# Estimates of the last chunk kept in SBUF, four of its products moved to ScalarE, and buffers and due times set anew

## The chip, the core and the metric

The kernel runs on one core of one Trainium2 chip. The metric is the device time of one execution in microseconds (us), as the median of several runs; a profiled execution gives the trace beside it. The engines are TensorE (PE), VectorE (DVE), ScalarE (ACT) and GpSimd (POOL); SyncE (SP) issues most DMAs here, POOL issues some. The on-chip memories are SBUF and PSUM; matmuls write to PSUM, and GpSimd works on SBUF here.

## The reference

Three stages on 12480 tokens of 128 channels:

```python
h   = mab(I, x)                      # softmax attention of 32 inducing points over all tokens
x1  = mab(x, h)                      # each token attends to the 32 results
h   = x1 @ w_in;  g = max(h, 0) + alpha * min(h, 0)
x2  = g @ w_out                      # first layer, 2048 wide
h   = x2 @ w_in2                     # second layer, 2048 wide
P   = a[0] + a[1]*h + a[2]*h*h + a[3]*h*h*h
Q   = 1 + |b[0]|*|h| + |b[1]|*h*h
out = (P / (Q + 1e-6)) @ w_out2
```

## The kernel before

The attention and the conversion of the weights fill the first 90 us or so; after that the work is cut into 26 chunks of 480 tokens (`W`), and each chunk into 8 units (`NU`), a unit being two blocks of 128 of the 2048 hidden channels, so a tile of 128x960. There are 208 units, numbered `k`; unit 200 is the first of the last chunk, and two units make a pair `j`. For each chunk the first layer runs on PE (`la1`, line 788; `lb`, line 801) with a relu on ACT (`r`, line 793), one chunk ahead of the second layer.

The second layer's rational function of unit `k` is a chain over four engines:

- PE: `l2` computes h into one of two PSUM buffers (lines 842 to 844, six matmuls).
- ACT: `s` = h*h (line 854). POOL: `A` = a3*s + a1 (line 863), and for a pair `B` = a2*s + a0 (line 868).
- DVE: `m` = h*A (line 875). For the pair POOL then issues a DMA, `P`, that adds B to m in SBUF (line 879); m is then the numerator.
- ACT: `z` = |b0*h| in place in PSUM (line 859). DVE: `q` = |b1|*s + z, into a tile `z` in SBUF (line 888): the denominator less a constant.
- ACT: `rho` = 1/sqrt(Q) (line 892) and `r0` = rho*rho (line 897), an estimate of 1/Q, into a PSUM tile `r` that exists once.
- DVE: one Newton step in place in the z tile, `ee` = Q*r0 (line 907), `r1` = (2 - ee)*r0 (line 911).
- POOL: `g` = m*z (line 922). For the last unit of each chunk DVE does it itself, as `g0` and `g` (lines 917 and 924).
- PE: `o` multiplies by the second weights (line 936) into the output of the chunk, which goes out by ACT, PE and a DMA at the chunk's end (`oa`, `ot`, `oy`, lines 948, 955, 962).

The order in which instructions are issued on each engine is fixed when the program is built. `graph` lists every operation with its engine, an assumed duration (`COST`), what it waits for, and a due time made from the table `DUE`; `arranged` then picks, engine by engine, what starts next. So a number in `DUE` changes nothing but the order. Before the first of these orders, a hand-written list (`START`) interleaves attention, conversion and the first chunk's first layer. The conversion of the weights (`cv`: lines 365, 369, 376 and 382, four steps on DVE for each of 16 pieces of 128x512, of which 13 steps are left over for the planned part) works in SBUF in the pool `cvr`. The pool `zz` takes over that memory, so a tile of `zz` can first be written when the last conversion step is done; the denominators z are tiles of `zz`, the numerators m (five buffers of a pair) are tiles of `ew`.

Of the kernel before, what the change touches and what calls it, by code (L numbers as in the profile page):

```python
# [43 lines left out]
DUE = dict(
    x2f=-0.45, la=-9.06, span=2.97, lb1=-13.61, at=-97.53, o=-23.76, o1=-13.46, ot=22.31, pack=12.69,
    l2=(29.67, 35.58, -79.83, -40.1, -11.09, -27.3, -24.5, -43.29),
    s=(-17.84, -32.0, -16.83, -26.56, -59.46, -97.25, -31.04, -54.94),
    A=(-63.73, -120.71, -103.15, -88.14, -48.47, -71.46, -128.35, -89.09),
    m=(-108.75, -22.15, -116.09, -46.72, -47.13, -42.75, -50.15, -148.19),
    B=(-54.95, -120.41, -105.91, -26.76, 36.86, -21.45, -83.45, 36.32),  # L50
    P=(187.3, 56.68, 20.63, 25.06, 67.81, -5.11, 38.88, -25.19),
    z=(-26.7, -63.52, -31.2, -26.94, 5.39, 24.47, 11.89, 15.71),
    q=(32.02, 39.1, 47.63, 65.87, 13.6, 133.96, 50.31, 70.75),
    rho=(36.83, 86.45, 150.83, 117.66, 71.04, 81.94, 112.77, 38.48),
    r0=(78.33, 29.52, 26.2, -49.91, 50.51, 19.63, -30.96, -28.81),
    ee=(62.9, 108.52, 89.98, 43.06, 77.86, 74.23, 43.3, 78.62),
    g0=(70.57, 75.02, 1.99, 84.61, 105.19, 73.56, 80.62, 149.83),
    g=(58.94, 3.2, 116.11, 8.69, 83.04, 10.67, 31.27, 107.91),
    r1=(40.2, 67.74, 21.19, 94.45, -8.56, 116.72, 111.67, -32.38),
    gp=(89.99, 44.35, 54.18, 117.38, 95.33, 178.76, 75.12, 95.23),  # L60
)
SLACK = 0.1
DVE_G = (7,)
MBUFS, ZBUFS = 5, 5
O_GATE, LB_GATE = 1, 6


def graph(NC, NU, due):
# [8 lines left out]
    LATER = ("r",)  # L77
    add(("x2a", 0), "A", C["cp"], [], 0)
    add(("x2b", 0), "V", 0.66, [("x2a", 0)], 0)
    for i in range(4):  # L80
# [4 lines left out]
    add(("w2l", 3), "G", 1.25, [], 1)
    for c in range(NC):
        at = c * CT
        x2 = at - due["x2f"]
# [13 lines left out]
        for j in range(2 * NU if c else 0):  # L102
            p, i = NU * c + j // 2, j % 2
            n = 2 * p + i
            t = x2 - (2 * NU - j) * TU / 2 * due["span"] - due["la"]
            add(("la1", p, i), "P", C["la1"], [("as_", c)], t, take="h1")
            add(("r", p, i), "A", C["r"], [("la1", p, i), ("lb", (n - 10) // 2, n % 2)], t + 0.3, give="h1")
# [3 lines left out]
            add(("lb", p, i), "P", C["lb"] + end, [("r", p, i)] + gate, t, take=None if j else "acc")  # L111
# [104 lines left out]
def tile_induced_attention__prelu_moe__rational_moe(  # L216
# [598 lines left out]
    def x2_f(c):  # L815
        xf = pools["rp2"].tile([P, W], F32, tag="xf", name="xf")
# [56 lines left out]
    def dve_m(k):  # L873
        Mm[k] = pair(MP, "ew", "m", MBUFS, k)
# [227 lines left out]
```

## Time and profile before

| | |
|---|---|
| median of 3 runs | 1214.61 us (1213.43 to 1216.71) |
| profiled execution | 1214.42 us, of which the span from first to last instruction is 1212.6 us |
| PE, ACT, DVE, POOL busy | 95%, 89%, 85%, 84% of the span |
| mean granted TensorE clock | 0.993 of full speed |

A busy share is a mean over stages that differ. In the rows further down a duration stands behind the start of an instruction, both in us from the span's start; what stands in square brackets is the idle time of the engine just before it and the instruction that ended it.

### The profile page before, as it was taken

Reading aid. Unit: us, or ns where it says so; the run is one execution under the profiler, and the core shown is the slowest. Engines: PE = TensorE matmul, PEld = TensorE weight load, DVE = VectorE, ACT = ScalarE, POOL = GpSimd, SP = SyncE. Lnnn points to the kernel's source line nnn. Section 1 sums busy time; section 2 is a strip of 40 time slices with the busy share of each in tenths; the row PEclk is TensorE's granted clock in tenths of the full one; section 3 lists DMA queues with packets and bytes.
Section 4 is the critical chain, followed back from the end, with each engine's and each line's share of the span. In section 5 each row is a group of like instructions: output and inputs, shape, how many; then the busy total and the mean of one; then the engine's idle time right before and its main releaser. Section 6 shows DMA issues by size and latency. Waiting matters only on the chain.

```text
span 1212.6 us, 12428 instructions
## 1 busy us (share of the span) xinstructions
PE 1150.4 (95%) x4137; PEld 685.3 (57%) x4137; DVE 1036.0 (85%) x1006; ACT 1073.9 (89%) x1485; POOL 1017.7 (84%) x693
## 2 busy tenths in 40 slices
PE   4998989999999999999999999999999999999996
PEld 3654555555655565655566555556555655565553
DVE  1796988889888888888988888998889889888996
ACT  3667989999989999999999999999999999999974
POOL 0135988998899998899989899988999898889895
PEclk9998999999999999999999999999999999999998
DMA  9801455454535545544554554454455545444553
GB/s 225 264 1 33 99 106 105 95 105 98 105 78 106 106 98 107 106 86 86 106 106 98 106 106 94 90 103 97 98 106 105 106 91 105 99 91 96 106 106 73
DMA packets 25260, 124.23 MB, mean 102 GB/s; under 512 B 2428, under 2 KB 6812, under 8 KB 24684
## 3 DMA queue, kind: packets, MB, share of 16 engines
q0 software_dynamic: 14976, 102.24, 42.2%
q1 hardware_dynamic: 9410, 18.25, 5.3%
q10 hardware_dynamic: 810, 2.95, 1.0%
q8 instruction: 33, 0.54, 0.2%
q14 instruction: 31, 0.25, 0.1%
HBM read 14.80 MB, written 6.39 MB: 17 GB/s over the span
## 4 chain that ended last, share of the span: by engine, by line
PE 60%; POOL 15%; DVE 9%; ACT 8%; issue 3%; DMA 3%; POOLq 0%; SPq 0%; ACTq 0%
PE oa L936 20%; PE xa L801 15%; POOL m L922 6%; PE h L842 5%; PE h L788 5%; PE h L844 5%; PE h L843 5%; POOL a L863 4%; POOL b L868 4%; DVE m L875 3%; ACT s L854 2%; DMA xs<-in_x_dram 2%; DVE z L888 2%; ACT r L897 2%; DVE z L907 2%
## 5 line engine op out<-in xcount | busy, mean ns | idle before, releaser
L922 POOL TENSOR_TENSOR m<-m,z 128x960 f32<-128x960 f32 x182 | 430.3, 2461 | 36.7 <-DVE z L911 35.3
L936 PE MATMUL oa<-m,w2o 128*128 128x480 f32 x832 | 373.1, 572 | 16.0 <-POOL b L868 7.8
L801 PE MATMUL xa<-r,w 128*128 128x480 f32 x832 | 376.2, 570 | 3.3 <-ACT o L948 2.8
L907 DVE SCALAR_TENSOR_TENSOR z<-z,r 128x960 f32<-128x960 f32 x208 | 239.3, 1151 | 85.2 <-ACT r L897 85.1
L863 POOL TENSOR_SCALAR a<-s,co 128x960 f32<-128x960 f32 x208 | 248.5, 1213 | 36.9 <-ACT s L854 35.1
L875 DVE TENSOR_TENSOR m<-h,a 128x960 f32<-128x960 f32 x208 | 235.9, 1154 | 39.0 <-POOL a L863 38.5
L793 ACT ACTIVATE r<-h 128x480 f32<-128x480 f32 x416 | 238.2, 573 | 20.0 <-PE h L788 16.8
L888 DVE SCALAR_TENSOR_TENSOR z<-s,bab,h 128x960 f32<-128x960 f32 x208 | 247.2, 1209 | 2.4 <-ACT h L859 1.9
L788 PE MATMUL h<-stk,wst 128*128 128x480 f32 x416 | 237.4, 572 | 10.2 <-ACT r L793 10.1
L936 PEld LDWEIGHTS oa<-m,w2o 128*128 128x128 f32 x832 | 156.2, 191 | 140.0 <-issue 110.0
L897 ACT ACTIVATE r<-rho 128x960 f32<-128x960 f32 x208 | 204.5, 983 | 30.8 <-DVE z L911 29.9
L801 PEld LDWEIGHTS xa<-r,w 128*128 128x128 f32 x832 | 155.4, 191 | 107.3 <-issue 87.7
L854 ACT ACTIVATE s<-h 128x960 f32<-128x960 f32 x208 | 197.0, 971 | 20.8 <-PE h L844 18.3
L911 DVE SCALAR_TENSOR_TENSOR z<-z,r 128x960 f32<-128x960 f32 x182 | 209.8, 1153 | 5.3
L859 ACT ACTIVATE h<-h 128x960 f32<-128x960 f32 x208 | 199.7, 965 | 13.3 <-DVE m L875 11.7
L892 ACT ACTIVATE rho<-z 128x960 f32<-128x960 f32 x208 | 207.8, 1004 | 3.5 <-DVE z L888 2.9
L868 POOL TENSOR_SCALAR b<-s,co 128x1920 f32<-128x1920 f32 x104 | 205.0, 1971 | 0.0
L842 PE MATMUL h<-xh,w2h 128*128 128x480 f32 x416 | 187.2, 450 | 6.5 <-DVE z L888 6.2
L844 PE MATMUL h<-xl,w2h 128*128 128x480 f32 x416 | 158.2, 380 | 0.0
L843 PE MATMUL h<-xh,w2l 128*128 128x480 f32 x416 | 158.0, 380 | 0.0
L788 PEld LDWEIGHTS h<-stk,wst 128*128 128x128 f32 x416 | 78.5, 189 | 114.9 <-ACT r L793 92.5
L879 POOL DMA_DIRECT2D m<-b x104 | 92.4, 888 | 33.2 <-POOL b L868 30.6
(132 smaller groups left out, 789.1 us busy)
## 6 DMA issues: line engine op xcount, KB each, us to landing
m<-b POOLq DMA_DIRECT2D x104, 960.0 KB, 6.7
out_dram<-y SPq DMA_DIRECT2D x25, 240.0 KB, 4.9
raw<-in_moe_w_in_dram SPq DMA_DIRECT2D x4, 1024.0 KB, 5.8
raw<-in_moe_w_out_dram SPq DMA_DIRECT2D x4, 1024.0 KB, 7.6
xs<-in_x_dram SPq DMA_DIRECT2D x7, 480.0 KB, 12.8
xs<-in_x_dram ACTq DMA_DIRECT2D x6, 480.0 KB, 9.4
out_dram<-y SPq DMA_DIRECT2D x2, 120.0 KB
ind<-in_inducing_dram SPq DMA_DIRECT2D x1, 16.0 KB, 1.7
```

The costliest lines, as they stand in the source:

```text
L788: nc.tensor.matmul(t[:, :W], lhsT=wst[:, f * P : (f + 1) * P], rhs=stk[c], start=True, stop=True)
L793: nc.scalar.activation(out=r, in_=h1s.pop((p, i))[:, :W], func=AF.Relu)
L801: nc.tensor.matmul(xacc[c][:, :W], lhsT=w1[:, f, :], rhs=rls.pop((p, i)), start=f == 0, stop=False)
L842: nc.tensor.matmul(t, lhsT=w2h[:, sl], rhs=xh, start=True, stop=False)
L863: nc.gpsimd.tensor_scalar(out=a, in0=S[k], scalar1=co[:, 3:4], scalar2=co[:, 1:2], op0=ALU.mult, op1=ALU.add)
L868: nc.gpsimd.tensor_scalar(out=b, in0=SP.pop(j), scalar1=co[:, 2:3], scalar2=co[:, 0:1], op0=ALU.mult, op1=ALU.add)
L875: nc.vector.tensor_tensor(out=Mm[k], in0=hs_[k][:, :, :W], in1=A_.pop(k), op=ALU.mult)
L888: nc.vector.scalar_tensor_tensor(out=Z[k], in0=S.pop(k), scalar=bab[:, 1:2], in1=z, op0=ALU.mult, op1=ALU.add)
L897: nc.scalar.activation(out=t[:, :, :W], in_=Rr.pop(k), func=AF.Square)
L907: nc.vector.scalar_tensor_tensor(out=Z[k], in0=Z[k], scalar=QC, in1=R0[k][:, :, :W], op0=ALU.add, op1=ALU.mult)
L922: nc.gpsimd.tensor_tensor(out=Mm[k], in0=Mm[k], in1=Z.pop(k), op=ALU.mult)
L936: nc.tensor.matmul(oacc[c][:, :W], lhsT=w2o[:, f, :], rhs=(G[k] if i == 0 else G.pop(k))[:, i], start=f == 0, stop=f == NF - 1)
```

## The change

- **Estimates of the last chunk.** For units 200 to 207 `act_r0` squares rho in place, in its SBUF tile, and `ee` and `r1` read it from there; the PSUM tile `r` is not used.
- **Last pair.** Units 206 and 207 get B added by two DVE instructions (`dve_p`), and `dma_p` is not issued for them. The last unit's product is `r1` and then m*z on DVE in place of `g0` and `g`.
- **Half of A on ScalarE.** For units 201, 203, 205 and 207 `pool_a` issues an ACT instruction.
- **Buffers.** The z tiles (five) move from `zz` to `ew`; of the five pair buffers of m, three stay in `ew` and two move to `zz`, as do the tiles `xf` and `o`. The planner now lets `q` of the first units run ahead of the last conversion steps, and makes `m` of pairs 3 and 4 of each five wait for them.
- **Due times.** All of `DUE` is new, with extra shifts (`xc`, `oc`, `uc`) for the first four and the last four chunks. `SPLIT` is empty and `R0_ODD` is false, so what hangs on them is not used.

```diff
+def r0_sbuf(k, NU, NUN):
+    return k >= NUN - NU or k % 2 and R0_ODD
+def a_act(k, NU, NUN):
+    return k % 2 and k >= NUN - NU
...
     def pool_a(k):
         a = pools["ew"].tile([P, 2, W], F32, tag="a", name="a", bufs=2)
-        nc.gpsimd.tensor_scalar(out=a, in0=S[k], scalar1=co[:, 3:4], scalar2=co[:, 1:2], op0=ALU.mult, op1=ALU.add)
+        if a_act(k, NU, NUN):
+            nc.scalar.activation(out=a, in_=S[k], func=AF.Identity, scale=co[:, 3:4], bias=co[:, 1:2])
+        else:
+            nc.gpsimd.tensor_scalar(out=a, in0=S[k], scalar1=co[:, 3:4], scalar2=co[:, 1:2], op0=ALU.mult, op1=ALU.add)
...
+    def dve_p(k):
+        j, i = divmod(k, 2)
+        nc.vector.tensor_tensor(out=Mm[k], in0=Mm[k], in1=B_[j][:, i], op=ALU.add)
...
     def dve_q(k):
-        Z[k] = pools["zz"].tile([P, 2, W], F32, tag="z", name="z", bufs=ZBUFS)
+        Z[k] = pools["ew"].tile([P, 2, W], F32, tag="z", name="z", bufs=ZBUFS)
...
     def act_r0(k):
+        if r0_sbuf(k, NU, NUN):
+            R0[k] = Rr.pop(k)
+            nc.scalar.activation(out=R0[k], in_=R0[k], func=AF.Square)
+            return
...
     def last_g(k):
-        if k % NU not in DVE_G:
-            nc.gpsimd.tensor_tensor(out=Mm[k], in0=Mm[k], in1=Z.pop(k), op=ALU.mult)
+        if not dve_g(k, NU, NUN):
+            eng = nc.gpsimd if k < NUN - 1 else nc.vector
+            eng.tensor_tensor(out=Mm[k], in0=Mm[k], in1=Z.pop(k), op=ALU.mult)
```

Between chunk 4 and chunk 21 the order on every engine stays as it was, but for a few swaps of neighbours. It moves at both ends.

**VectorE at the start of the planned part.** The names are those of the text above; h_ and r_ are PSUM tiles, cvt, raw and w2o belong to the conversion. Before, from the first numerator on:

```order
L875 TENSOR_TENSOR m<-h_1044,a 128x960
L376 SCALAR_TENSOR_TENSOR cvt<-raw,cvt 128x512
L875 TENSOR_TENSOR m<-h_1063,a 128x960
L382 SCALAR_TENSOR_TENSOR w2o<-raw,cvt 128x512
L365 TENSOR_SCALAR cvt<-cvt 128x512
L369 TENSOR_SCALAR cvt<-cvt 128x512
L376 SCALAR_TENSOR_TENSOR cvt<-raw,cvt 128x512
L382 SCALAR_TENSOR_TENSOR w2o<-raw,cvt 128x512
L888 SCALAR_TENSOR_TENSOR z<-s,bab,h_1044 128x960
L888 SCALAR_TENSOR_TENSOR z<-s,bab,h_1063 128x960
L907 SCALAR_TENSOR_TENSOR z<-z,r_1151 128x960
```

Now (lines 917, 934 and 957 are what 875, 888 and 907 were; 403, 407, 414 and 420 are the four conversion steps):

```order
L917 TENSOR_TENSOR m<-h_1041,a 128x960
L414 SCALAR_TENSOR_TENSOR cvt<-raw,cvt 128x512
L420 SCALAR_TENSOR_TENSOR w2o<-raw,cvt 128x512
L917 TENSOR_TENSOR m<-h_1061,a 128x960
L934 SCALAR_TENSOR_TENSOR z<-s,bab,h_1041 128x960
L934 SCALAR_TENSOR_TENSOR z<-s,bab,h_1061 128x960
L403 TENSOR_SCALAR cvt<-cvt 128x512
L407 TENSOR_SCALAR cvt<-cvt 128x512
L414 SCALAR_TENSOR_TENSOR cvt<-raw,cvt 128x512
L420 SCALAR_TENSOR_TENSOR w2o<-raw,cvt 128x512
L957 SCALAR_TENSOR_TENSOR z<-z,r_1133 128x960
```

The two denominators stand ahead of the last piece's four steps, and the second numerator behind one more step. On ScalarE three relus (line 793) stood between the second absolute value (line 859) and the first reciprocal root (line 892, with a table load ahead of it); now one does.

**VectorE at the end, the last instructions of units 205 to 207.** Before; the tiles r_ are in PSUM:

```order
L907 SCALAR_TENSOR_TENSOR z<-z,r_9071 128x960
L875 TENSOR_TENSOR m<-h_9055,a 128x960
L888 SCALAR_TENSOR_TENSOR z<-s,bab,h_9031 128x960
L888 SCALAR_TENSOR_TENSOR z<-s,bab,h_9055 128x960
L911 SCALAR_TENSOR_TENSOR z<-z,r_9071 128x960
L907 SCALAR_TENSOR_TENSOR z<-z,r_9097 128x960
L911 SCALAR_TENSOR_TENSOR z<-z,r_9097 128x960
L907 SCALAR_TENSOR_TENSOR z<-z,r_9105 128x960
L917 TENSOR_TENSOR r_9105<-m,r_9105 128x2x480
L924 SCALAR_TENSOR_TENSOR m<-z,r_9105 128x960
```

Now; rho, m, b and z are all SBUF tiles (line 929 is `dve_p`, line 961 what 911 was, line 973 the product m*z):

```order
L929 TENSOR_TENSOR m<-m,b 128x960
L934 SCALAR_TENSOR_TENSOR z<-s,bab,h_9039 128x960
L929 TENSOR_TENSOR m<-m,b 128x960
L934 SCALAR_TENSOR_TENSOR z<-s,bab,h_9027 128x960
L957 SCALAR_TENSOR_TENSOR z<-z,rho 128x960
L961 SCALAR_TENSOR_TENSOR z<-z,rho 128x960
L957 SCALAR_TENSOR_TENSOR z<-z,rho 128x960
L961 SCALAR_TENSOR_TENSOR z<-z,rho 128x960
L957 SCALAR_TENSOR_TENSOR z<-z,rho 128x960
L961 SCALAR_TENSOR_TENSOR z<-z,rho 128x960
L973 TENSOR_TENSOR m<-m,z 128x960
```

All 16 instructions of lines 957 and 961 in the last chunk read `z` and `rho`, two SBUF tiles, where those of lines 907 and 911 read one SBUF and one PSUM tile. From the first numerator of unit 200 to the last product DVE has 38 instructions, where it had 36.

**GpSimd at the end, from the B of units 202 and 203.** Before:

```order
L868 TENSOR_SCALAR b<-s,co 128x1920
L879 DMA m<-b 128x1920
L922 TENSOR_TENSOR m<-m,z 128x960
L863 TENSOR_SCALAR a<-s,co 128x960
L922 TENSOR_TENSOR m<-m,z 128x960
L863 TENSOR_SCALAR a<-s,co 128x960
L868 TENSOR_SCALAR b<-s,co 128x1920
L879 DMA m<-b 128x1920
L922 TENSOR_TENSOR m<-m,z 128x960 x2
L863 TENSOR_SCALAR a<-s,co 128x960 x2
L868 TENSOR_SCALAR b<-s,co 128x1920
L879 DMA m<-b 128x1920
```

Now (904, 909, 921 and 973 are what 863, 868, 879 and 922 were):

```order
L909 TENSOR_SCALAR b<-s,co 128x1920
L973 TENSOR_TENSOR m<-m,z 128x960
L921 DMA m<-b 128x1920
L904 TENSOR_SCALAR a<-s,co 128x960
L973 TENSOR_TENSOR m<-m,z 128x960
L909 TENSOR_SCALAR b<-s,co 128x1920
L921 DMA m<-b 128x1920
L973 TENSOR_TENSOR m<-m,z 128x960
L904 TENSOR_SCALAR a<-s,co 128x960
L909 TENSOR_SCALAR b<-s,co 128x1920
L973 TENSOR_TENSOR m<-m,z 128x960 x4
```

One A of each pair and the last DMA are gone; behind these rows three products were left before, and four of the last row's are now.

## Rows read from the trace of the kernel before

**Rows 1.** The page: busy us, share of the span, instructions.

```profile
PE   1150.4 (95%) x4137; PEld 685.3 (57%) x4137; DVE 1036.0 (85%) x1006; ACT 1073.9 (89%) x1485; POOL 1017.7 (84%) x693
```

**Rows 2.** Busy time of each engine by stretch; PEclk is TensorE's granted clock.

```profile
90.00:120.00 30.00, 25.31 (x72) 13.67 (x70) 20.58 (x28) 23.65 (x37) 17.76 (x16) 0.89 0.16 33
120.00:150.00 30.00, 26.88 (x89) 15.80 (x89) 27.07 (x25) 28.69 (x40) 28.42 (x20) 1.00 0.49 99
150.00:200.00 50.00, 46.07 (x152) 27.39 (x151) 43.53 (x41) 44.39 (x60) 45.46 (x30) 1.00 0.51 104
400.00:500.00 100.00, 99.20 (x328) 59.26 (x327) 89.98 (x81) 95.06 (x130) 90.43 (x64) 1.00 0.49 100
1190.00:1200.00 10.00, 4.96 (x10) 2.03 (x9) 8.27 (x8) 6.13 (x7) 8.39 (x5) 0.74 0.49 98
```

**Rows 3.** Timeline of VectorE, 100 to 116 us: start, duration, instruction, idle before.

```profile
101.41 0.96 DVE L376 SCALAR_TENSOR_TENSOR cvt<-raw,cvt 128x512 uint32<-128x512 uint32 x1
102.29 1.14 DVE L875 TENSOR_TENSOR m<-h,a 128x960 f32<-128x960 f32 x1
103.36 1.36 DVE L382 SCALAR_TENSOR_TENSOR w2o<-raw,cvt 128x512 uint32<-128x512 uint32 x1
...
106.28 0.69 DVE L382 SCALAR_TENSOR_TENSOR w2o<-raw,cvt 128x512 uint32<-128x512 uint32 x1
106.89 2.33 DVE L888 SCALAR_TENSOR_TENSOR z<-s,bab,h 128x960 f32<-128x960 f32 x2
114.85 1.16 DVE L907 SCALAR_TENSOR_TENSOR z<-z,r 128x960 f32<-128x960 f32 x1 [5.63 <-ACT r L897]
```

**Rows 4.** Timeline of ScalarE, 110 to 116 us.

```profile
110.92 0.57 ACT L793 ACTIVATE r<-h 128x480 f32<-128x480 f32 x1 [0.57 <-PE h L788]
111.51 1.28 ACT L892 ACT_TABLE_LOAD   x1
112.81 1.01 ACT L892 ACTIVATE rho<-z 128x960 f32<-128x960 f32 x1
113.84 0.98 ACT L897 ACTIVATE r<-rho 128x960 f32<-128x960 f32 x1
114.75 0.95 ACT L854 ACTIVATE s<-h 128x960 f32<-128x960 f32 x1
```

**Rows 5.** Timeline of GpSimd, 100 to 130 us.

```profile
100.69 1.14 POOL L863 TENSOR_SCALAR a<-s,co 128x960 f32<-128x960 f32 x1 [0.39 <-ACT s L854]
101.81 2.37 POOL L868 TENSOR_SCALAR b<-s,co 128x1920 f32<-128x1920 f32 x1
...
115.82 1.13 POOL L863 TENSOR_SCALAR a<-s,co 128x960 f32<-128x960 f32 x1 [10.21 <-ACT s L854]
...
128.96 1.95 POOL L868 TENSOR_SCALAR b<-s,co 128x1920 f32<-128x1920 f32 x1
```

**Rows 6.** The chain that ended last, 1194 us to the end.

```profile
1194.14 6.65 DMA m<-b
...
1203.18 3.61 PE oa L936 x8
```

**Rows 7.** Timeline of GpSimd, 1166 to 1203 us.

```profile
1166.70 1.14 POOL L863 TENSOR_SCALAR a<-s,co 128x960 f32<-128x960 f32 x1
...
1194.14 0.88 POOL L879 DMA_DIRECT2D m<-b  x1 [0.52 <-POOL b L868]
...
1200.92 2.21 POOL L922 TENSOR_TENSOR m<-m,z 128x960 f32<-128x960 f32 x1 [1.45 <-DMA m<-b]
```

**Rows 8.** Timeline of VectorE, 1160 to 1205 us.

```profile
1160.18 2.26 DVE L875 TENSOR_TENSOR m<-h,a 128x960 f32<-128x960 f32 x2 [0.62 <-POOL a L863]
...
1169.12 1.15 DVE L907 SCALAR_TENSOR_TENSOR z<-z,r 128x960 f32<-128x960 f32 x1
...
1203.69 1.15 DVE L924 SCALAR_TENSOR_TENSOR m<-z,r 128x960 f32<-128x960 f32 x1
```

**Rows 9.** Line 907, all of it: duration in ns, least, median and greatest.

```profile
L907 DVE SCALAR_TENSOR_TENSOR z<-z,r x208: 1143/1153/1157, 114.9 to 1201.4; 128x960 f32<-128x960 f32 x104
```

More of the change, by code (lines that the diff above doesn't have):

```diff
@@ L44 @@
 DUE = dict(
[L45 to L51, printed above, removed]
@@ L63, with dve_g @@
+    ee=(43.61, 76.08, -7.14, 32.8, 53.24, 41.16, 13.78, 95.05),
+    g0=(81.94, 35.06, -18.35, 99.1, 149.33, 48.25, 103.16, 184.03),
+    g=(-18.17, -128.72, 2.8, -164.79, 12.02, -99.61, -42.73, 10.01),
+    r1=(17.37, -29.06, -9.69, 6.85, -82.06, 118.68, 64.68, 13.0),
+    gp=(119.04, 23.24, 105.33, 143.13, 90.81, 226.13, 91.72, 94.68),
+)
+SLACK = 0.09
+SPLIT = ()
 DVE_G = (7,)
-MBUFS, ZBUFS = 5, 5
+MBUFS, ZBUFS, RBUFS = 5, 5, 10
+R0_ODD = False
 O_GATE, LB_GATE = 1, 6
+def dve_g(k, NU, NUN):
+    return k % NU in DVE_G and k < NUN - 1
@@ L76, in graph, with freed, edge @@
     C, NUN, CT = COST, NC * NU, NU * TU
-    LATER = ("r",)
+    LATER, LATE = ("r",), [("conv",)]
+    def freed(n):
+        return [("lb", (n - RBUFS) // 2, n % 2)]
+    def edge(key, c):
+        return due[key][c] if c < 4 else due[key][c - NC + 8] if c >= NC - 4 else 0.0
     add(("x2a", 0), "A", C["cp"], [], 0)
@@ L87, in graph @@
         at = c * CT
-        x2 = at - due["x2f"]
+        x2 = at - due["x2f"] + edge("xc", c)
         if c > 1:
@@ L106, in graph @@
             add(("la1", p, i), "P", C["la1"], [("as_", c)], t, take="h1")
-            add(("r", p, i), "A", C["r"], [("la1", p, i), ("lb", (n - 10) // 2, n % 2)], t + 0.3, give="h1")
+            add(("r", p, i), "A", C["r"], [("la1", p, i)] + freed(n), t + 0.3, give=None if j in SPLIT else "h1")
+            split = j in SPLIT
+            if split:
+                add(("rl", p, i), "V", C["rl"], [("r", p, i)], t + 0.9, give="h1")
             gate = [("r", p + LB_GATE // 2, LB_GATE % 2)] if j == 0 else [("lb", (n - 1) // 2, 1 - i)]
@@ L110, in graph @@
             t = x2 - (2 * NU - j) * due["lb1"]
-            add(("lb", p, i), "P", C["lb"] + end, [("r", p, i)] + gate, t, take=None if j else "acc")
+            add(("lb", p, i), "P", C["lb3" if split else "lb"] + end, [("rl" if split else "r", p, i)] + gate, t, take=None if j else "acc")
         if c:
@@ L815, in x2_f @@
     def x2_f(c):
-        xf = pools["rp2"].tile([P, W], F32, tag="xf", name="xf")
+        xf = pools["zz"].tile([P, W], F32, tag="xf", name="xf", bufs=1)
         nc.scalar.copy(xf, xacc.pop(c)[:, :W])
@@ L846, in pair @@
     def pair(store, pool, tag, bufs, k):
-        if k % 2 == 0:
+        if k // 2 not in store:
             store[k // 2] = pools[pool].tile([P, 2, 2, W], F32, tag=tag, name=tag, bufs=bufs)
@@ L862, in pool_a @@
         a = pools["ew"].tile([P, 2, W], F32, tag="a", name="a", bufs=2)
[L863 removed]
+        if a_act(k, NU, NUN):
+            nc.scalar.activation(out=a, in_=S[k], func=AF.Identity, scale=co[:, 3:4], bias=co[:, 1:2])
+        else:
+            nc.gpsimd.tensor_scalar(out=a, in0=S[k], scalar1=co[:, 3:4], scalar2=co[:, 1:2], op0=ALU.mult, op1=ALU.add)
         A_[k] = a
@@ L873, in dve_m @@
     def dve_m(k):
-        Mm[k] = pair(MP, "ew", "m", MBUFS, k)
+        left = k // 2 % MBUFS < 3
+        Mm[k] = pair(MP, "ew" if left else "zz", "m", 3 if left else MBUFS - 3, k)
         nc.vector.tensor_tensor(out=Mm[k], in0=hs_[k][:, :, :W], in1=A_.pop(k), op=ALU.mult)
@@ L944, in out_a @@
     def out_a(c):
-        o = pools["rp2"].tile([P, W], F32, tag="o", name="o", bufs=1)
+        o = pools["zz"].tile([P, W], F32, tag="o", name="o", bufs=1)
         acc = oacc.pop(c)
```

61 lines of the change are left out of this document (37 added, 24 removed).

## The prediction, made before the change was run

> **What bounds the kernel now.** I read the page first: PE is busy 95% of the span, the other three 84 to 89% [rows 1]. Then the stretches: between 400 and 500 us PE is busy 99.20 of 100 [rows 2], so the middle is PE's, and a change that leaves its order alone gives nothing there. PE is not full at two places. From 90 to 120 us it idles 4.7 of 30 us at a mean granted clock of 0.89, from 120 to 200 us 7.0 of 80; at the end, between 1190 and 1200 us, it works 4.96 of 10 at 0.74 [rows 2]. Only there can time come or go, and there the timelines of single engines say what is late.
>
> At the start, DVE has the first two denominators behind the last conversion step: they run from 106.89 to 109.22 [rows 3]. ACT takes them up only after three relus: the table load for the reciprocal root starts at 111.51, the third `s` at 114.75 [rows 4], and POOL, idle for 10.21 us, starts the third A at 115.82 [rows 5]. From there to the third B at 128.96 POOL has little idle time, and it is what PE's second-layer work waits for.
>
> At the end, the chain runs through the last DMA that adds B to m (1194.14, 6.65 us), POOL's product of unit 206 (waits 1.45 us for it, ends at 1203.13), and eight matmul rows from 1203.18 to 1206.79 [rows 6, 7]. DVE is nearly as late: its last product ends at 1204.84 [rows 8], 1.95 us ahead of PE's last row. So the removal of the DMA alone could gain little: DVE stands right behind.
>
> **The start, step by step.** I follow the new order with the old durations. The conversion step that starts at 101.41 takes 0.96 us where one of its kind takes 0.69 undisturbed [rows 3]: POOL's A holds it until 101.83, and 0.54 us later it ends. POOL's B, issued at 101.81, takes 2.37 us against 1.95 for a later one [rows 5], as it lets that step finish first. The next such step, issued at 103.36 while B runs until 104.18, ends 0.54 us after B, at 104.72 [rows 3, 5]. These steps have two inputs in SBUF; the numerator at 102.29 has one of its inputs in PSUM, lies in the same stretch of B and takes its plain 1.14 us [rows 3]. In the new order that last step stands ahead of the second numerator. It still ends at 104.72, so the numerator ends at about 105.8 instead of 103.4, the denominators at 106.9 and 108.1, only 1.1 us earlier than before. But on ACT only one relu is left between them and the table load: absolute value (taken as long as an `s`) to 106.8, relu 0.57 to 107.4, load 1.28 to 108.7, root 1.0 to 109.7, square 1.0 to 110.7, third `s` 0.95 to 111.6. Before, that `s` ended at 115.70 [rows 4]; the third A starts at 111.7 instead of 115.82: 4.1 us.
>
> POOL's order up to the third B is now A, A, B, DMA, product, A, product, A. Its work is 4 x 1.14 + 1.95 + 0.88 + 2 x 2.21 = 11.8 us [rows 5, 7]. It waits twice: 0.5 us for the fourth `s` (root and `s` behind the third: 113.3), and for the fifth. That one needs PE's matmuls of unit 4, and these the third denominator, which DVE reaches behind two numerators (the later ends 1.15 us after POOL's A at 114.5) and one Newton step, so at 118.0; with a first-layer group and its own six matmuls PE is through at 120.3, `s` at 121.4, where POOL is ready at 119.2: 2.2 us. So the third B starts at 126.2, not 128.96 [rows 5]. I take this **2.8 us** as the gain at the start: PE has the idle time to give it back from, since it has 11.7 us of it before 200 us. Bounds: 1 us, by the denominators alone, and 4.1 us, by the third A.
>
> The four DVE steps behind the denominators cost nothing while the first estimate is under way: DVE sat idle for 5.63 us there [rows 3]. The moved buffers and the swaps among chunks 0 to 3 and 22 to 25 I cost at nothing: PE covers them (99.20 of 100). Were the cover gone, a swap would cost up to one instruction, about 1 us.
>
> **The end, step by step.** First what is taken away. POOL loses four A of 1.14 us and one DMA issue of 0.88 [rows 7]; ACT, busy 6.13 of 10 us [rows 2], takes the A's beside its own work. ACT's square no longer waits for the PSUM tile. DVE gets two instructions more. From 1160.18 on it has 38, which back to back (about 1.12 us from start to start) would end at 1202.8 instead of 1204.84. With no collisions the end would gain at most 2.0 us.
>
> Now what is added. In all 208 cases of line 907 the duration lies between 1143 and 1157 ns, though POOL is busy beside it most of the time: one input in SBUF, one in PSUM, and no collision [rows 9]. In the last chunk `ee` and `r1` of eight units, the two sums and the last product have two SBUF inputs: 19 instructions. The only operations of that kind beside POOL's work in the trace are the conversion steps, and each that meets a POOL instruction waits for its end, or makes the next one wait [rows 3, 5]. The trace does not show it for f32 instructions of 960 elements. From below: no collision, 0. From above: DVE's 19 and POOL's readers exclude each other altogether. The nearest rows are the conversion steps, and all of them that I could place against POOL's times agree with exclusion, so I take that.
>
> The Trainium skill says the same in "SBUF — State Buffer", section "Who interferes with whom": a VectorE instruction with two SBUF inputs contends with a GpSimd instruction that reads SBUF, and the one that comes second is blocked until the first is done, while one with at most one SBUF input is left alone. By that rule the sum is the one I take; by the plain f32 rows of line 907 it would be the first rival.
>
> The price. From `ee` of unit 200 on (before at 1169.12 [rows 8]; now it is due while POOL runs the A of unit 202, from about 1167.5, where the old one ran from 1166.70 [rows 7]) POOL has three A of 1.14, three B of 1.95 and seven products of 2.21 us: 24.7 us. DVE's 19 at 1.07 are 20.3 us. In single file they end at 1167.5 + 24.7 + 20.3 = 1212.5. On the way come stretches in which neither is at it: the two denominators 206 and 207 among the sums, when POOL has run dry since it waits for `r1` of unit 205; 2 x 1.15 = 2.3 us. So the last product ends at 1214.8, not 1204.84; with PE's 1.95 us behind it as before, the end is **9.9 us later**. The DMA of the last pair is then no loss or gain: its numerators are ready long before POOL and DVE come to them. Bounds: 5.8 us, if each blocked instruction saves its start-up (1.01 us for 960 elements at the pace of the steps' 0.54 for 512, 1.81 for B, 2.16 for a product) and no stretch is empty; 12 us, if PE's last rows run at half the clock and DVE loses every tie.
>
> **Sum.** The profiled execution took 1214.42 us, 0.2 below the median of the runs. 1214.42 - 2.8 + 9.9 = **1221.5 us**. With the bounds 5.8 - 4.1 and 12 - 1 it lies between 1216 and 1225.5.
>
> **Rivals.** *No collision* (faster): f32 instructions out of two SBUF tiles run beside POOL as those of line 907 do. For it: 1157 ns at most in 208 cases; against it: those read PSUM, and the steps that read SBUF twice do wait. Then DVE ends 2.0 us earlier; but PE, which stood idle before the last products (clock 0.74 [rows 2]), has unit 205's matmuls close before the end at a low clock, and I leave 1.3 us. 1214.42 - 2.8 - 1.3 = 1210.3 us. My price is 9.9 + 1.3 = 11.2 us for 19 instructions, 0.59 each: where fewer than 7 of them meet a POOL instruction, the end costs less than the start gains.
>
> *Collisions, but no gain at the start*: DVE's second numerator is 2.4 us later than before, and if PE or POOL wait for something else after 120 us, the lead is lost there. 1214.42 + 9.9 = 1224.3 us.
>
> *Collisions that fall into gaps*: DVE and POOL wait for each other anyway (POOL's products wait for `r1`, DVE's `ee` for ACT's squares), and a block that lies in such a wait costs nothing. If 12 of the 19 waits fell there, the end would be 7 x 0.59 - 1.3 = 2.8 us later and the sum the old time, 1214.4 us. Against it: DVE had few idle times left from 1160 on (4.7 of 44.7 us, 36 instructions at 1.11 subtracted).
>
> **Chances.** Forecast 0.60, no collision 0.16, no gain at the start 0.12, into gaps 0.12. A measurement of this kernel can tell about 0.3%, 3.6 us, from no change. Slower by more: most of the forecast (0.50) and the second rival (0.12), 0.62. Faster by more: most of the first rival (0.12) and a little of the others (0.03), 0.15. Within: 0.23. The range reaches down to the first rival's slow side, 1211, and up to 1225: outside it lie about 0.12 below and 0.06 above.
>
> **What would show it.** Start: the third `s` on ACT ends about 4 us earlier than 115.70 and the third B starts near 126.2; the second numerator on DVE ends near 105.8. End: durations of `ee` and `r1` in the last chunk of up to 3 us where 1157 ns was the greatest, products and B's on POOL that take about 1 us more than 2.21 and 1.94, alternating with them; the last product of DVE some 12 us behind where its no-collision time would put it, and PE's last rows right behind it. I am wrong if those durations stay near 1.15 us, if the start gains nothing, or if the middle (PE's 99 of 100) loses time by the new order.

## The result, and the profile after

The changed kernel takes 1222.34 us (median of 7 runs, 1219.07 to 1223.75) where the kernel before takes 1214.5 beside it; the ratio is 1.0058 with an interval of 1.0046 to 1.0070. It is slower. The profiled execution took 1220.15 us, 1218.4 of it the span, against 1214.42 and 1212.6 before.

The busy line of the page (us, share of the span, instructions) first:

```profile
PE 1152.8 (95%) x4137; PEld 685.8 (56%) x4137; DVE 1048.5 (86%) x1008; ACT 1079.3 (89%) x1489; POOL 1021.1 (84%) x688
```

DVE has two instructions more than before [rows 1] and is busy 12.5 us longer. Where, the stretches show (busy us of PE, PEld, DVE, ACT and POOL, then TensorE's granted clock, DMA share and GB/s):

```profile
90.00:120.00 30.00, 26.43 (x87) 15.50 (x87) 24.85 (x34) 26.91 (x43) 22.18 (x18) 0.94 0.23 46
120.00:150.00 30.00, 27.61 (x92) 15.81 (x90) 27.31 (x26) 27.96 (x38) 28.05 (x19) 1.00 0.43 87
...
1190.00:1200.00 10.00, 5.60 (x8) 2.22 (x8) 9.98 (x7) 2.93 (x4) 6.77 (x3) 0.66 0.00 0
1200.00:1210.00 10.00, 5.05 (x8) 1.85 (x8) 9.88 (x6) 2.99 (x3) 6.05 (x2) 0.66 0.00 0
```

From 90 to 150 us PE does 1.85 us more than before [rows 2]: the start gained. From 1190 to 1210 us DVE is busy 19.86 of 20 us with only 13 instructions, 1.5 us each.

**The start.** The timelines of DVE, ACT and POOL:

```profile
106.06 2.32 DVE L934 SCALAR_TENSOR_TENSOR z<-s,bab,h 128x960 f32<-128x960 f32 x2
...
107.62 1.28 ACT L938 ACT_TABLE_LOAD   x1
...
110.87 0.95 ACT L892 ACTIVATE s<-h 128x960 f32<-128x960 f32 x1
...
111.94 1.14 POOL L904 TENSOR_SCALAR a<-s,co 128x960 f32<-128x960 f32 x1 [3.70 <-ACT s L892]
...
126.12 1.95 POOL L909 TENSOR_SCALAR b<-s,co 128x1920 f32<-128x1920 f32 x1
```

The table load starts at 107.62 instead of 111.51, the third A at 111.94 instead of 115.82, the third B at 126.12 instead of 128.96 [rows 4, 5]. These are less than the gain, since this execution was late before the change came into play. ACT's first relu of the first layer, far ahead of it, and POOL's low half of the last chunk's input (`xl`), behind the middle, stand in the two traces at (relu and low half of before, then of after):

```profile
61.71 0.57 ACT L793 ACTIVATE r<-h 128x480 f32<-128x480 f32 x1 [0.80 <-PE h L788]
...
1153.12 1.50 POOL L828 TENSOR_TENSOR xl<-xf,xh 128x480 fp32r<-128x480 f32 x1
```

```profile
63.20 0.57 ACT L831 ACTIVATE r<-h 128x480 f32<-128x480 f32 x1 [0.80 <-PE h L826]
...
1149.81 1.49 POOL L866 TENSOR_TENSOR xl<-xf,xh 128x480 fp32r<-128x480 f32 x1
```

From relu to low half it is 1091.41 us before and 1086.61 after, 4.8 less; the relu itself came 1.49 us later.

**The end.** From that low half to the end of DVE's last product, which I call the tail, it is 51.72 us before (to 1204.84 [rows 8]) and 60.87 after (to 1210.68). DVE's groups on the z tiles and the numerators from 1157 us on, and POOL's product and A (duration in ns: least, median, greatest; an estimate in SBUF appears as `rho`, one in PSUM as `r`):

```profile
L957 DVE SCALAR_TENSOR_TENSOR z<-z,rho x8: 1144/1147/1902, 1164.6 to 1205.3; 128x960 f32<-128x960 f32 x8
L961 DVE SCALAR_TENSOR_TENSOR z<-z,rho x8: 1159/1868/3093, 1167.5 to 1206.4; 128x960 f32<-128x960 f32 x8
L929 DVE TENSOR_TENSOR m<-m,b x2: 2044/2495/2946, 1191.7 to 1195.7; 128x960 f32<-128x960 f32 x2
...
L973 POOL TENSOR_TENSOR m<-m,z x8: 2200/2599/3133, 1158.5 to 1205.5; 128x960 f32<-128x960 f32 x8
...
L904 POOL TENSOR_SCALAR a<-s,co x3: 1137/2133/3022, 1164.3 to 1185.7; 128x960 f32<-128x960 f32 x3
```

Where 1157 ns was the greatest for `ee` [rows 9], `r1` now takes up to 3093. How they meet shows best at the very end (DVE, then POOL):

```profile
1201.09 1.15 DVE L957 SCALAR_TENSOR_TENSOR z<-z,rho 128x960 f32<-128x960 f32 x1
1202.28 3.05 DVE L961 SCALAR_TENSOR_TENSOR z<-z,rho 128x960 f32<-128x960 f32 x1
1205.25 1.14 DVE L957 SCALAR_TENSOR_TENSOR z<-z,rho 128x960 f32<-128x960 f32 x1
1206.43 3.05 DVE L961 SCALAR_TENSOR_TENSOR z<-z,rho 128x960 f32<-128x960 f32 x1
1209.52 1.16 DVE L973 TENSOR_TENSOR m<-m,z 128x960 f32<-128x960 f32 x1
...
1201.25 3.06 POOL L973 TENSOR_TENSOR m<-m,z 128x960 f32<-128x960 f32 x1 [4.48 <-DVE z L961]
1205.47 3.00 POOL L973 TENSOR_TENSOR m<-m,z 128x960 f32<-128x960 f32 x1 [1.16 <-DVE z L961]
```

POOL's product of unit 205 is issued at 1201.25, while DVE's `ee` of 206 is running; it takes 0.85 us more than 2.21, which fits a wait for that `ee`, which ends at 1202.24. Then `r1` of 206 is issued at 1202.28 and waits for the product, which ends at 1204.31; 1.02 us later `r1` ends, at 1205.33. Its end releases the next product, the next `ee` is already running, and the same again. Two engines do the work of one. The chain that ended last (start, us, what) now ends on these instructions and one unit's matmuls, where it had a DMA, POOL's product and eight matmul rows [rows 6]:

```profile
1202.28 3.05 DVE z L961
...
1206.43 3.06 DVE z L961
...
1209.52 1.17 DVE m L973
...
1210.73 1.89 PE oa L987 x4
```

### The profile page after: what moved, and what is told of

It is laid out like the page before. It is cut to its first block, busy times and chain, and to the rows that moved or that the text cites. A ratio compares the mean times of both kernels' runs of the same rounds, so it can differ in the third digit from the quotient of the medians.

```text
span 1218.4 us, 12428 instructions
## 1 busy us (share of the span) xinstructions
PE 1152.8 (95%) x4137; PEld 685.8 (56%) x4137; DVE 1048.5 (86%) x1008; ACT 1079.3 (89%) x1489; POOL 1021.1 (84%) x688
## 4 chain that ended last, share of the span: by engine, by line
PE 51%; POOL 19%; DVE 13%; ACT 9%; issue 5%; DMA 2%; SPq 0%; ACTq 0%; POOLq 0%
PE oa L987 17%; PE xa L839 13%; POOL m L973 8%; POOL a L904 5%; PE h L826 5%; PE h L880 5%; PE h L882 4%; PE h L881 4%; POOL b L909 4%; DVE m L917 4%; DVE z L957 2%; DVE z L934 2%; DMA xs<-in_x_dram 2%; ACT s L892 2%; DVE z L961 2%
## 5 line engine op out<-in xcount | busy, mean ns | idle before, releaser
L957 DVE SCALAR_TENSOR_TENSOR z<-z,r 128x960 f32<-128x960 f32 x200 | 230.1, 1150 | 72.7 <-ACT r L947 72.4
L826 PE MATMUL h<-stk,wst 128*128 128x480 f32 x416 | 233.5, 562 | 7.5 <-ACT r L831 7.2
L947 ACT ACTIVATE r<-rho 128x960 f32<-128x960 f32 x200 | 196.4, 982 | 23.8 <-DVE z L961 23.1
L909 POOL TENSOR_SCALAR b<-s,co 128x1920 f32<-128x1920 f32 x104 | 209.3, 2012 | 0.6 <-ACT s L892 0.6
L961 DVE SCALAR_TENSOR_TENSOR z<-z,r 128x960 f32<-128x960 f32 x175 | 201.7, 1153 | 5.1
```

The costliest lines, as they stand in the source:

```text
L826: nc.tensor.matmul(t[:, :W], lhsT=wst[:, f * P : (f + 1) * P], rhs=stk[c], start=True, stop=True)
L909: nc.gpsimd.tensor_scalar(out=b, in0=SP.pop(j), scalar1=co[:, 2:3], scalar2=co[:, 0:1], op0=ALU.mult, op1=ALU.add)
L957: nc.vector.scalar_tensor_tensor(out=Z[k], in0=Z[k], scalar=QC, in1=R0[k][:, :, :W], op0=ALU.add, op1=ALU.mult)
L961: nc.vector.scalar_tensor_tensor(out=Z[k], in0=Z[k], scalar=2.0, in1=R0.pop(k)[:, :, :W], op0=ALU.subtract, op1=ALU.mult, reverse0=True)
```

## The experiments

Ten kernels. Besides their times I read two stretches of each one's profiled execution: relu to low half, and the tail. The tail depends little on how late an execution got going and on what the start gained: it is 51.7 us before and 51.0 in e3, 60.9 with the change and 61.0 in e4, pairs with the same end and different starts. It is not the whole end, though. What follows DVE's last product to the end of the span takes 7.6 to 8.4 us in nine of the traces, and 9.1 to 9.4 in e1, e4 and e5.

| kernel | first relu | low half | DVE's last product ends | relu to low half | tail |
|---|---|---|---|---|---|
| before | 61.71 | 1153.12 | 1204.84 | 1091.4 | 51.7 |
| changed | 63.20 | 1149.81 | 1210.68 | 1086.6 | 60.9 |
| e1, estimates in PSUM | 62.98 | 1149.32 | 1209.64 | 1086.3 | 60.3 |
| e2, before, estimates in SBUF | 62.69 | 1153.38 | 1214.23 | 1090.7 | 60.9 |
| e3, changed start alone | 61.76 | 1149.58 | 1200.57 | 1087.8 | 51.0 |
| e4, changed end alone | 60.47 | 1151.36 | 1212.33 | 1090.9 | 61.0 |
| e5, a PSUM tile in the estimates' place | 61.91 | 1148.69 | 1200.25 | 1086.8 | 51.6 |
| e6, odd estimates in SBUF | 63.46 | 1150.35 | 1208.19 | 1086.9 | 57.8 |
| e7, e3 and A on ScalarE | 65.21 | 1153.28 | 1208.50 | 1088.1 | 55.2 |
| e8, e3 and sums on VectorE | 59.73 | 1145.76 | 1200.79 | 1086.0 | 55.0 |
| e9, e3 and odd estimates in SBUF | 61.04 | 1147.14 | 1205.75 | 1086.1 | 58.6 |
| e10, e3 and one estimate in SBUF | 61.05 | 1148.55 | 1199.68 | 1087.5 | 51.1 |

My theory: DVE's instructions with two SBUF operands and POOL's instructions exclude each other (a collision, where one has to wait for the other), and that is the whole loss at the end; the start gains about 3 us. Rival: the end's new order, with A on ScalarE and the sums on VectorE, costs it by itself.

### e1: the changed order, estimates in PSUM

```diff
     def act_r0(k):
-        if r0_sbuf(k, NU, NUN):
+        if False:
```

> The changed kernel with its order kept instruction for instruction; only the last chunk's estimates go to PSUM, as before the change, so that the 16 ee and r1 of its units read one operand from PSUM. Theory (collisions: two SBUF operands on VectorE against GpSimd, price 0.6 us or more an instruction): 16 of the 19 colliding instructions go, the tail shrinks by some 8 us and the lead of 3.3 us from the start stays: 1211 to 1214 us, faster than before or equal to it. Rival (the new order, the due times, A on ScalarE and the sums on VectorE cost the end its 9 us): no change from the changed kernel, 1221 to 1223. In between, 1215 to 1219: both have a share.

Measured: 1219.94 us (9 runs; before 1213.95 on this chip), ratio 1.0046, 1.0031 to 1.0061. My theory's number is missed and the rival's nearly met. But the trace shows that the experiment exchanged one thing for another. DVE's two Newton lines from 1145 us on (busy us, mean ns, then idle time just before them):

```profile
L961 DVE SCALAR_TENSOR_TENSOR z<-z,r 128x960 f32<-128x960 f32 x11 | 12.7, 1152 | 0.3
L957 DVE SCALAR_TENSOR_TENSOR z<-z,r 128x960 f32<-128x960 f32 x11 | 12.7, 1150 | 6.9 <-ACT r L947 6.9
```

Every one of these durations is back at 1.15 us: the collisions of `ee` and `r1` are gone. In their place `ee` waits 6.9 us for ACT's square (5.5 of them in the last eight units), which waits for `r1` of the unit ahead to free the single PSUM tile. The new order needs the estimates' own buffers. This run decides nothing between the theories, so e5 was made.

### e2: the order of before, estimates in SBUF

```diff
     def act_r0(k):
+        if k >= NUN - NU:
+            R0[k] = Rr.pop(k)
+            nc.scalar.activation(out=R0[k], in_=R0[k], func=AF.Square)
+            return
```

> The kernel before with its order kept; only the last chunk's eight estimates are squared in place in SBUF. Theory (collisions): the 16 ee and r1 of the last chunk now hold off GpSimd's A, B and product instructions and are held off by them: 6 to 11 us slower, 1220 to 1225. Rival (the order of the end is what costs): within 1.5 us of before, 1213 to 1216. Squaring on ScalarE into SBUF instead of PSUM is the same instruction, so it should cost nothing by itself under either.

Measured: 1223.93 us (6 runs; before 1213.95), ratio 1.0086, 1.0066 to 1.0106: 10 us slower by the medians, near the upper end of the theory's range. Nothing but the place of eight estimates differs. (The colliding instructions here are 17: eight `ee`, seven `r1`, and the last unit's two products.) DVE's rows:

```profile
L911 DVE SCALAR_TENSOR_TENSOR z<-z,rho x8: 1144/1276/2283, 1169.3 to 1208.8; 128x960 f32<-128x960 f32 x8
L915 DVE SCALAR_TENSOR_TENSOR z<-z,rho x7: 1157/1982/3082, 1171.5 to 1207.7; 128x960 f32<-128x960 f32 x7
```

The tail is 9.1 us longer than before's, as long as the changed kernel's.

### e3 and e4: one half of the change each

The planned order of before and that of after hold the same operations in their first 2240 places, so they can be spliced there. e3 also keeps before's end in the code (estimates in PSUM, adding DMA, all A on POOL); e4 is the other way about.

```diff
...
-    for name, *args in arranged(NC, NU):
+    new, old = arranged(NC, NU), OLD["arranged"](NC, NU)
+    cut = 2240
+    for name, *args in new[:cut] + old[cut:]:
```

> The changed start (denominators ahead of the last conversion steps, their own buffers) with the end of the kernel before: estimates in PSUM, the last pair summed by DMA, all A on GpSimd. Theory (the start gives 2.8 to 3.3 us, and everything after it moves forward by that): 1211 to 1212 us. Rival (the end does not use an earlier start, or the start gives nothing): 1214 to 1215.

Measured: 1210.38 us (12 runs; before 1213.95), ratio 0.9970, 0.9958 to 0.9981. The start alone gains 3.6 us by the medians (2.3 to 5.1 by the interval), a little more than the theory's 1211 to 1212 us asked for.

> The start's order of before (with the changed kernel's buffers) and the whole end of the changed kernel. Theory (the end costs 9 us whatever the start does): 1223 to 1225 us. If the changed end only costs because the start runs ahead of it (an interaction), 1214 to 1219. This run and the one with the start alone should add up to the changed kernel's difference: minus 3 plus 9.

Measured: 1224.09 us (6 runs), ratio 1.0092, 1.0070 to 1.0113: 10.1 us slower by the medians. The two add up to 6.5; the change measured 1.0058, about 7 us. e4 has the changed kernel's buffers and before's start order, and its 1090.9 us from relu to low half are before's (1091.4): the buffers alone gain hardly anything, the order does.

### e5: the changed kernel with a fixed PSUM tile as second operand

This kernel leaves out the last chunk's division: `FIX[0]` is a PSUM tile left from an earlier unit, read in the place of the estimate.

```diff
     def dve_e(k):
+        if k >= NUN - NU:
+            nc.vector.scalar_tensor_tensor(
+                out=Z[k], in0=Z[k], scalar=R0[k][:, 0, 0:1], in1=FIX[0][:, :, :W], op0=ALU.add, op1=ALU.mult
+            )
+            return
...
     def dve_r1(k):
...
+        if k >= NUN - NU:
+            R0.pop(k)
+            nc.vector.scalar_tensor_tensor(
+                out=Z[k], in0=Z[k], scalar=2.0, in1=FIX[0][:, :, :W], op0=ALU.subtract, op1=ALU.mult, reverse0=True
+            )
+            return
```

> The changed kernel, order and buffers kept, the square still written to SBUF by ScalarE; but the 16 ee and r1 of the last chunk read, in place of the estimate, one PSUM tile that is left from an earlier unit and that nobody rewrites (ee takes one number of the estimate, so it still waits for ScalarE). The last chunk's values are therefore not the reference's. This takes away both the second SBUF operand and the wait for the single PSUM buffer that the run with the estimates in PSUM has put in its place (DVE's ee waited 6.9 us for ScalarE there). Theory (two SBUF operands against GpSimd): the 7.9 us that L957 and L961 take above 1.15 each, and some of GpSimd's, go; 1212 to 1215. Rival (the new order costs the end its 9 us in itself): 1219 to 1223.

Measured: 1213.79 us (11 runs; before 1213.51 on this chip), ratio 1.0002, 0.9993 to 1.0011. The theory's range, and far from the rival's. `ee` (L960) and `r1` (L969):

```profile
L960 DVE SCALAR_TENSOR_TENSOR z<-z,rho,r x8: 1203/1208/1209, 1163.5 to 1196.7; 128x960 f32<-128x960 f32 x8
L969 DVE SCALAR_TENSOR_TENSOR z<-z,r x8: 1144/1153/1155, 1165.7 to 1197.9; 128x960 f32<-128x960 f32 x8
```

The tail is 51.6 us, within 0.2 of before's. Same order, same A on ScalarE, same sums on DVE; only the second SBUF operand of 16 instructions is gone, and with it 9.3 us of the tail, 0.58 each. So the rival falls as the main cause. But it isn't refuted altogether, since the tail isn't all of e5's end. What ends it is TensorE, with the output rows of three units behind POOL's product of unit 205:

```profile
1196.80 6.79 PE L999 MATMUL oa<-m,w2o 128*128 128x480 f32 x12 [4.83 <-POOL m L985]
```

TensorE had stood idle for 4.83 us, and between 1197 and 1200 us its granted clock is 0.50, the lower of its two levels (1.2 GHz): a row takes 1.01 us there and 0.57 from 1201 on. What follows DVE's last product takes 9.17 us, 1.5 more than in the changed kernel, so of the 9.3 us 7.8 are left at the span's end; by the ratios of the two kernels it is 0.56%, 6.8 us. And this execution was the fastest of e5's eleven, 2.6 us below their median. By the medians e5 is 0.3 us above before, where e3, with the same start, is 3.6 below: 3.9 us of the loss stay with the changed end without these operands. Against e3's trace 1.8 of them show, 0.6 in the tail and 1.2 behind it; where the other 2 arise isn't known.

### e6: every other estimate in SBUF

```diff
-        if r0_sbuf(k, NU, NUN):
+        if k >= NUN - NU and k % 2:
```

> The changed kernel, order kept; only the odd four of the last eight units have their estimates in SBUF, the even four in PSUM. Eight instructions collide instead of 16, and the PSUM buffer has a unit's time more to come free. Theory with 0.6 us a collision and hardly a wait for the buffer: 1216 to 1219. If waits for the buffer come in the same measure as collisions go, or if the order alone costs it: 1220 to 1223.

Measured: 1217.39 us (12 runs; before 1213.51), ratio 1.0022, 1.0010 to 1.0035: the middle of the theory's range. But this doesn't measure the price of a collision. The tail is 6.3 us above e5's; DVE's rows in it:

```profile
L917 DVE TENSOR_TENSOR m<-h,a 128x960 f32<-128x960 f32 x8 | 9.1, 1155 | 3.5 <-POOL a L904 1.8 <-ACT a L902 1.7
L957 DVE SCALAR_TENSOR_TENSOR z<-z,r 128x960 f32<-128x960 f32 x7 | 8.0, 1149 | 2.5 <-ACT r L947 2.5
...
L961 DVE SCALAR_TENSOR_TENSOR z<-z,rho 128x960 f32<-128x960 f32 x4 | 6.5, 1631 | 0.1
L957 DVE SCALAR_TENSOR_TENSOR z<-z,rho 128x960 f32<-128x960 f32 x4 | 5.3, 1317 | 0.0
```

The eight instructions that read two SBUF tiles take 2.6 us more than 1.15 each. DVE's idle time is 6.8 us against e5's 2.8: 1.1 more for the PSUM tile's square and 3.0 more for A's on POOL and ACT.

### e7 and e8: the other two parts of the changed end, alone, on top of e3

e7 issues the odd units' A on ScalarE right behind their squares `s`, and no longer on GpSimd; e8 puts two DVE sums in the place of the last adding DMA.

```diff
         nc.scalar.activation(out=S[k], in_=hs_[k][:, :, :W], func=AF.Square)
+        if a_act(k, NU, NUN):
+            pool_a(k)
...
```

```diff
...
+        if (name, *args) == ("P", NUN // 2 - 1):
+            dve_p(NUN - 2)
+            dve_p(NUN - 1)
+            continue
         OPS[name](*args)
```

> The kernel with the changed start and the end of before, and of the changed end one part: the odd units' A of the last chunk on ScalarE, right behind their squares. Four A of 1.14 us leave GpSimd; VectorE's numerators waited 1.4 us for A in the last 60 us. If the part is worth anything: 1208.5 to 1210. If it costs (ScalarE's other work is pushed back by 1.2 us four times): 1211 to 1213. My guess: within 1 us of the kernel with the changed start alone, 1209.5 to 1211.4.

Measured: 1213.92 us (12 runs, 1209.82 to 1217.84; before 1213.51), ratio 0.9996, 0.9984 to 1.0008. My guess is missed: the part costs some 3 us against e3, and 4.2 in the tail. One of the four places (ACT, then DVE):

```profile
1180.25 1.19 ACT L1081 ACTIVATE a<-s,co 128x960 f32<-128x960 f32 x1
1181.34 0.95 ACT L1126 ACTIVATE r<-rho 128x960 f32<-128x960 f32 x1
...
1182.33 1.15 DVE L1136 SCALAR_TENSOR_TENSOR z<-z,r 128x960 f32<-128x960 f32 x1 [1.68 <-ACT r L1126]
```

The A pushes the square back that DVE is about to wait for; over the tail DVE waits 7.3 us for squares where e3 waits 3.7. ScalarE has idle time in the mean, but not there.

> The kernel with the changed start and the end of before, and of the changed end one part: the last pair's numerators summed by VectorE (two instructions with two SBUF operands) in place of the adding DMA. The 1.46 us for which GpSimd's last product waited for the DMA go; two sums of 1.15 us stand in VectorE's row, and by the theory each meets GpSimd's products and takes about 2. Theory: 1.5 to 4 us above the kernel with the changed start alone, 1212 to 1214.5. Rival (the DMA was the end's limit, as the change seems to take it to be): 1208 to 1210.

Measured: 1213.27 us (11 runs; before 1213.51), ratio 0.9997, 0.9988 to 1.0006: in the theory's range. The two sums and the product that they meet (DVE, POOL):

```profile
1187.38 3.27 DVE L1106 TENSOR_TENSOR m<-m,b 128x960 f32<-128x960 f32 x2
...
1186.35 2.22 POOL L1150 TENSOR_TENSOR m<-m,z 128x960 f32<-128x960 f32 x1
```

The first sum waits until 1188.57, when the product ends; the pair takes 3.27 us instead of some 2.2. The tail is 4.0 us longer than e3's: some 2.2 are the two sums themselves, 1.1 their waits. The adding DMA was not what held this end, and replacing it costs.

### e9 and e10: fewer estimates in SBUF, with the order of before at the end

The edit, against e3:

```diff
-        if False:
+        if k >= NUN - NU and k % 2:
```

> The kernel with the changed start and the end of before; of the last eight units the odd four have their estimates in SBUF. In the order of before, nine of VectorE's instructions (four ee, three r1, the product with the estimate and the last product) then read two SBUF operands, and the waits for the single PSUM buffer go, of which this order has some 2.6 us among the last eight units. Theory at 0.53 to 0.6 us a collision (9.1 us over the 17 of the run that puts all eight into SBUF): the stretch from the last low half on GpSimd to VectorE's last product grows from 51.0 to between 53 and 55 us, the time to 1212 to 1215. If the waits that go weigh as much as the collisions that come: 1209.5 to 1211.5.

Measured: 1219.19 us (12 runs; before 1215.30 on this chip), ratio 1.0032, 1.0020 to 1.0045. A miss: the tail grew by 7.6 us, not 2 to 4. The row that shows why (DVE, POOL):

```profile
1178.91 3.70 DVE L1134 SCALAR_TENSOR_TENSOR z<-z,rho 128x960 f32<-128x960 f32 x1
...
1179.06 2.52 POOL L1150 TENSOR_TENSOR m<-m,z 128x960 f32<-128x960 f32 x1
```

This one `ee` pays 2.55 us: the product's row begins 0.15 us behind it, and yet the product goes first, and `ee` ends 1.03 us after it. A flat price for a collision is a mean over cases from 0 to 2.6 us. DVE also waits 3.9 us for PSUM squares over the tail, no less than e3's 3.7: what the buffers gave was lost again, I think because the squares wait for delayed DVE work; no run shows that apart.

e10 is the same edit with `k == NUN - 2`, one estimate.

> The same kernel with one estimate alone in SBUF, that of the last unit but one, so that the last unit's square has not to wait for its predecessor's PSUM buffer. One wait of 1.1 us goes, two instructions collide (with the products of the units 204 and 205). Theory: minus 1.1, plus 2 x 0.55, so within 1 us of the kernel with the changed start alone: 1209.5 to 1211.5, and the waited time before VectorE's last ee gone from its row.

Measured: 1209.78 us (6 runs; before 1215.30), ratio 0.9954, 0.9937 to 0.9971. The time is as expected, and the best of all kernels here with e3, from which it can't be told (0.9958 to 0.9981). Its one `ee` beside the two products:

```profile
1192.47 2.69 DVE L1134 SCALAR_TENSOR_TENSOR z<-z,rho 128x960 f32<-128x960 f32 x1 [0.90 <-ACT rho L1121]
...
1189.46 4.67 POOL L1150 TENSOR_TENSOR m<-m,z 128x960 f32<-128x960 f32 x2
```

It waits for the products, which end at 1194.13, and ends 1.03 us later, at 1195.16; what this costs, 1.54 us, the waits that went give back, and the tail is 51.1 against 51.0. Of the two collisions expected only this one came: `r1` behind it takes 1.16 us.

## Why the prediction was right

**The end** was forecast at +9.9 us and came at +9.15 in the tail, and what follows the last product takes 7.72 us to the end of the span against 7.76. The price, 0.59 us for each of 19 instructions or 11.2 in all, is found again as excess over 1.15 us: by the means of 2.05 us, 1.24 and 2.50, eight `r1` 7.2 us, eight `ee` 0.7, two sums 2.7, the last product none: 10.6 in all. With its two further instructions DVE is busy 12.3 us longer in the tail and idle 3.2 less (3.7 where it was 6.9, since 3.3 of its waits for PSUM squares are gone), which makes the 9.1. The forecast let POOL run dry for 2.3 us, waiting for `r1` of unit 205; it did so for 4.48, and `ee` and `r1` of that unit ran in it untouched. The forecast's reading is that they exclude POOL's readers altogether. The rows show it, and that it is the main cause is shown by e2 (before's order with nothing else changed: +9.1 in the tail) and e5 (the changed order with 16 of the 19 gone: back at 51.6). The exclusion is what the Trainium skill's "SBUF — State Buffer", section "Who interferes with whom", states; it also says that the order of issue decides who blocks, and here the trace agrees in most rows (POOL waits 0.85 us for an `ee` under way, `r1` behind it for the product) but, by the rows' starts, not in e9's `ee` at 1178.91, which POOL overtook, nor here in the changed kernel (DVE, then POOL):

```profile
1183.59 3.09 DVE L961 SCALAR_TENSOR_TENSOR z<-z,rho 128x960 f32<-128x960 f32 x1
1186.61 1.15 DVE L957 SCALAR_TENSOR_TENSOR z<-z,rho 128x960 f32<-128x960 f32 x1
...
1185.67 3.02 POOL L904 TENSOR_SCALAR a<-s,co 128x960 f32<-128x960 f32 x1
```

The A's row begins 0.94 us ahead of that `ee`, which begins 0.07 us before the `r1` in front of it ends; yet `ee` takes its plain 1.15 us, and the A ends 0.93 us behind it.

**Who pays.** I had `ee` and `r1` in mind alike. In the changed kernel it is mostly `r1` that pays (7.2 of 7.9 us): an instruction of POOL's that has waited for an `ee` starts to run when that `ee` ends, and `r1`, whose row begins 0.03 to 0.04 us later, is blocked. In e2 `ee` pays 1.8 of 7.9 us, and in e9 3.4 of 5.3.

**The start** was forecast at 2.8 us, between 1 and 4.1, and was sized too small, by 1.3 us. From relu to low half it is 1091.0 us in the mean of the three traces with before's start order and 1086.9 in the nine with the changed one: 4.1 us. The term that failed is the conversion step ahead of the second numerator. I let it end 0.54 us after POOL's B; in the new order it met the shorter second A instead (which ends at 104.54, the step at 105.07). DVE's pair of denominators ended at 108.38. Less the late beginning of 1.49 us that is 106.89; I had 108.1. Counted in the same way the third A starts at 110.45 and the third B at 124.63, 1.2 and 1.6 us ahead of the forecast's 111.7 and 126.2. The profiled execution of after hid part of this behind its late beginning, which the forecast had no term for.

**The sum.** 1214.42 + 1.49 - 4.80 + 9.15 = 1220.26, against 1220.15 profiled; the forecast, 1221.5, is 0.8 below the median. That it lies so near is in part luck: this median stands 2.2 us above its profiled execution, where before's stood 0.2 above. Against the profile it was off by 2.0 us at the start and 0.75 at the end, both to the high side, and by 1.49 to the low side for the late beginning. The prediction gives two ranges, 1216 to 1225.5 by its bounds and 1211 to 1225 with the first rival's; the median lies in both.

**The middle** was costed at nothing. From the third A to the low half it is 1037.30 us before and 1037.87 after, 0.6 more.

**The parts costed at nothing at the end.** The adding DMA's removal was called no loss or gain beside the collisions of its sums; e8 shows that sums and removal together cost 4.0 us of tail in before's order. A on ScalarE was costed at nothing since ACT was idle; in before's order that is wrong (e7: +4.2), and not far off in the changed one, where e5 has DVE waiting for no square of the last eight units and for no A of ScalarE (in e6, with the same order, it waits 1.7 us for A's of ScalarE). In the changed kernel both stand inside the 9.15.

**The rivals.** No collision: refuted by the durations above. No gain at the start: refuted by e3. Collisions that fall into gaps: DVE had none left from 1190 to 1210 us, 9.98 and 9.88 of 10 us busy, and over the whole tail it is idle for 3.7 us with the collisions and for 2.8 without 16 of them (e5), so none of their cost was taken from its idle time.

What stays open: the 2 us by which e5 is slower than its trace explains; why POOL went first in e9 though its row begins second, and DVE in the changed kernel; and what it is worth to share the denominators' memory with the conversion in the new order, which was not tried, since they are written while the conversion still uses it.

## What to carry to other kernels

Before an operand is moved from PSUM to SBUF to get rid of a wait, count which VectorE instructions then read SBUF twice, and what GpSimd does beside them: here 16 such instructions cost 9.3 us of the tail, some 7 to 8 of the time, and the wait for squares that they did away with had come to 3.6 us (DVE's idle time before line 907 of the kernel before, from 1166 us on). An experiment that undoes one part of a change may bring back the very wait that the part removed (e1); leave the order and take only the operand away (e5) to see its price. And compare stretches between two marks of the trace rather than ends: the tails of the changed kernel and of e4, which has the same end, agree within 0.1 us, where the first relu wanders by 5. But look behind the second mark too: e4 is 1.7 us longer than the changed kernel there.

## What was not expected of the hardware

- A scalar operand in SBUF (128x1) beside one PSUM operand does not collide: in e5 `ee` with such a scalar takes 1203 to 1209 ns in all eight cases, in six of which one of POOL's instructions runs beside it, and `q` (one of its operands in PSUM, a scalar from `bab`) 1198 to 1218 in all 208 of the changed kernel.
- A blocked `ee` or `r1` ends 1.00 to 1.03 us after POOL's instruction (1205.33 after 1204.31; 1195.16 after 1194.13; in e9 1182.61 after 1181.58), where an unblocked one takes 1.15: so only some 0.12 to 0.15 us of it seem to be done while it waits.
- The first relu stands between 59.73 and 65.21 us in twelve traces, though the instructions up to there are the same in all twelve kernels. e7's profiled execution, 65.21, is also its slowest (1217.84), e8's, 59.73, its fastest (1210.93); but e5's and e9's are also the fastest of theirs, at 61.91 and 61.04.
